# Gate and value products of an attention and gated-MLP kernel: seven block products in place of eight, on spans of 512 tokens

## The chip, the cores and the metric

The kernel runs on one core of a Trainium2 chip, as one program with one launch. Its time is device microseconds; the time before is the median of three runs, 1030.5 us (1030.05 to 1031.13). The engines of the core are named as the profile names them: PE is the matrix engine (PEld its weight loads), DVE the vector engine, ACT the scalar engine, POOL the general engine, SP the engine that issues DMAs. Each takes its own instructions in the order of the program, and waits at an instruction whose inputs or buffers aren't ready.

## The reference

```
q_s = softmax of q over head_dim;  k_s = softmax of k over the sequence
kv  = einsum('bhsd,bhse->bhde', k_s, v)            # 8 batches, 8 heads, 576 tokens, head_dim 64
x   = einsum('bhsd,bhde->bhse', q_s, kv)           # laid out as 4608 tokens x 512
out = (sigmoid(x @ w_gate) * (x @ w_val)) @ w_out  # 512 -> 1536 -> 512
```

The inputs are float32, and the three weights arrive as 64-bit floats' bit patterns and are narrowed to float32 on the chip.

## The kernel before

The 4608 tokens are worked off in 12 spans of `T = 384` (`w`), and in each span the 1536 hidden columns in 12 blocks of 128 (`j`). For a span and a block, `g1` makes gate and value of the block for all tokens of the span (two PSUM tiles `gv` of 384 columns, summed over four blocks of 128 input columns), ACT takes the sigmoid, DVE multiplies (`g_mul`), and `g2` adds the block's part of the output into one PSUM tile `acc` for each 128 tokens. `g2` of a block is issued behind `g1` of the next one.

**Split products.** From the second span on, each factor is held as two float32r parts, a rounded one (`hi`) and the rest (`lo`), and a product is three matmuls: hi by hi, lo by hi, hi by lo. The first span (w = 0) is computed in plain float32 instead, since the weights only arrive and are narrowed while it runs: `narrow_low`, `narrow_sign`, `narrow_abs`, `narrow_join` (lines 84 to 107, on DVE and ACT) for block j + 2, then `w_split` (line 128) makes its two parts, the `hi` on ACT, the `lo` on POOL. Gate and value weights then stay in SBUF in two parts for all spans. The output weights stay in float32, and `split_wo` (line 419) makes their two parts again for every span and block, ACT for `hi` (line 422), POOL for `lo` (line 423).

**Attention** of the next span is spread over the blocks of the running one by `side(n, j)` (line 502): row maxima, exponentials and sums of q (`qn_*`), q again in the other layout (`qT_*`, with maxima and reciprocals sent through DRAM and spread over partitions as `q_b`), and, if a new batch begins, `k_sub`, `k_exp`, `k_mm`, `k_done`. `x_mm` (line 362) makes the next span's x from it in three float32r matmuls for each head pair; where a span covers two batches it makes two parts, each at least 256 tokens wide, and `x_ev` (line 403) splits x into `x_hi` and `x_lo`.

The order on each engine is that of the code (`manual_schedule`): per block `g1`, `split_wo`, `g_mul`, the split of the product, `g2` of the block ahead, `side`. PSUM has eight tiles of 512 columns: three `gv`, three `acc`, two `at` for attention. With three `gv` tiles a new `g1` needs the tile that was read one block ago.

```
for s, rh in ((0, xh), (0, xl), (1, xh)):
    nc.tensor.matmul(
        ps[i], lhsT=w_hl[j][:, i, s, ks], rhs=rh[:, kt], ...
```

Of the kernel before, what the change touches and what calls it, by code (L numbers as in the profile page):

```python
# [17 lines left out]
P = 128  # L18
# [3 lines left out]
T = 384  # L22
# [4 lines left out]
NK = DM // P  # L27
G = P // H
NC = 4
# [4 lines left out]
NS = 7  # L34
EPS = 1e-9


@with_exitstack
def attn_moe(ctx: ExitStack, tc: tile.TileContext, qf, qn, qT, k, kT, v, wg, wv, wo, out):
# [15 lines left out]
    nc.vector.memset(kv_0, 0.0)
    v_ones = [const.tile([P, NP, VW], F32, name=f"v_sb{i}") for i in range(2)]
# [3 lines left out]
    ctx.enter_context(tc.manual_schedule())  # L60

# [37 lines left out]
    def narrow_abs(raw, w):  # L99
        nc.scalar.activation(w, words(raw)[:, :, 1].bitcast(F32), AF.Abs, scale=2.0 ** -112)  # L100

    def narrow_join(raw, w):
        bits = w.bitcast(I32)
        nc.vector.scalar_tensor_tensor(  # L104
            out=bits, in0=bits, scalar=3, in1=words(raw)[:, :, 0],
            op0=ALU.logical_shift_left, op1=ALU.bitwise_or,
        )

    w_32 = {}

    def w_bits(j, jo):

        raws = [w_raw[i].rearrange("p n e -> p (n e)") for i in (j,) if i in w_raw]
        raws += [wo_raw[i] for i in (jo,) if i in wo_raw]
        for f in (narrow_low, narrow_sign):
            for raw in raws:
                f(raw)

    def w_abs(j):
        w_32[j] = [ring.tile([P, DM], F32, name="ring") for _ in range(2)]  # L120
        for n in range(2):
            narrow_abs(w_raw[j][:, n], w_32[j][n])

    def w_join(j, *parts):
        for n in parts or range(2):
            narrow_join(w_raw[j][:, n], w_32[j][n])

    def w_split(j):
        w = w_32[j]
        w_hl[j] = hl = wpool.tile([P, 2, 2, DM], F32R, name="w_hl", tag=f"w{j}")  # L130
        for n in range(2):
            nc.scalar.copy(out=hl[:, n, 0], in_=w[n])  # L132
            nc.gpsimd.tensor_tensor(  # L133
                out=hl[:, n, 1], in0=w[n], in1=hl[:, n, 0].bitcast(F32), op=ALU.subtract
            )

    def wo_abs(j):
        narrow_abs(wo_raw[j], wo_32[:, j])

    def wo_join(j):  # L140
        narrow_join(wo_raw.pop(j), wo_32[:, j])
# [705 lines left out]
```

## Time and profile before

| | before |
|---|---|
| median of three runs | 1030.5 us |
| the profiled execution's own time | 1030.21 us |
| its span, first to last instruction | 1028.4 us |
| mean granted PE clock | 0.992 |
| matmuls in the profile | 5202 |
| HBM read and written | 80.87 MB and 9.70 MB |

Times inside the profile are counted from the first instruction. A matmul's duration in it is longer than the step from its start to the next one's start, because matmuls overlap; what a row of matmuls costs is read from starts. A plain float32 matmul of the code stands in the profile as two matmuls of its width. An entry such as "L443 ... gv<-x_hi,w_hl" is line 443, written tile, read tiles.

### The profile page before, as it was taken

To read this page: it belongs to the slowest core of one execution; us is meant where nothing else is said; L and a number is where in the kernel's file an instruction comes from. 1 tells how busy PE (TensorE), PEld (TensorE's weight loads), DVE (VectorE), ACT (ScalarE), POOL (GpSimd) and SP (SyncE) were. 2 spreads that over 40 slices of the span, in tenths; PEclk is the share of its full clock that TensorE was granted. 3 is DMA by queue.
4 is the path that set the end of the run, shared out by engine and by line. 5 is a ranking of instruction groups with operands and counts; after the bars stand their busy time and mean duration, and the time that the engine had idled before them with its cause. 6 is when DMAs were issued, how large, how long until landed. Compare 5 with 4: busy or idle time off the path is not lost.

```text
span 1028.4 us, 13887 instructions
## 1 busy us (share of the span) xinstructions
PE 1007.8 (98%) x5202; PEld 901.7 (88%) x5202; DVE 482.4 (47%) x835; ACT 361.0 (35%) x670; POOL 387.9 (38%) x335
## 2 busy tenths in 40 slices
PE   6988999999999999999999999999999999999998
PEld 5545579999999999999999999999999999999997
DVE  7899943435444443343353443344444443343222
ACT  3544533324324334324324232332442342332211
POOL 3346243434425523525425433334432541351221
PEclk8998999999999999999999999999999999999999
DMA  9934301233214201305315311124223420120000
GB/s 328 366 86 175 113 32 62 77 95 119 80 52 146 86 16 47 101 23 155 99 51 155 88 47 47 61 64 134 88 83 82 126 73 8 57 68 1 32 1 31
DMA packets 71746, 91.47 MB, mean 89 GB/s; under 512 B 13440, under 2 KB 53376, under 8 KB 71680
## 3 DMA queue, kind: packets, MB, share of 16 engines
q1 hardware_dynamic: 71680, 90.60, 28.0%
q8 instruction: 41, 0.67, 0.3%
q14 instruction: 25, 0.20, 0.1%
HBM read 80.87 MB, written 9.70 MB: 88 GB/s over the span
## 4 chain that ended last, share of the span: by engine, by line
PE 88%; DVE 5%; DMA 3%; issue 2%; SPq 1%; ACT 0%; DVEq 0%; ACTq 0%
PE gv L443 54%; PE acc L482 27%; PE at L207 3%; PE at L375 3%; PE gv L436 2%; DVE ring L104 1%; PE acc L476 1%; DMA x_lent<-wo_in 1%; DVE w_raw L87 1%; DMA w_raw<-wv_in 1%; DMA x_lent<-k_in 1%; SPq L185 1%; DMA lent<-k_in 0%; DVE x_lent L87 0%; DVE x_lent L94 0%
## 5 line engine op out<-in xcount | busy, mean ns | idle before, releaser
L443 PE MATMUL gv<-x_hi,w_hl 128*128 128x384 f32 x2112 | 561.9, 336 | 0.0
L443 PEld LDWEIGHTS gv<-x_hi,w_hl 128*128 128x128 f32 x2112 | 383.8, 188 | 4.4 <-issue 0.5
L423 POOL TENSOR_TENSOR wo_lo<-wo,wo_hi 128x512 fp32r<-128x512 f32 x132 | 170.2, 1289 | 520.4 <-ACT wo_hi L422 465.6
L443 PE MATMUL gv<-x_lo,w_hl 128*128 128x384 f32 x1056 | 353.8, 335 | 0.0
L454 DVE TENSOR_TENSOR sig<-gv,sig 128x384 f32<-128x384 f32 x144 | 80.4, 558 | 426.4 <-PE gv L443 421.8
L449 ACT ACTIVATE sig<-gv 128x384 f32<-128x384 f32 x144 | 70.8, 492 | 408.3 <-PE gv L443 386.2
L443 PEld LDWEIGHTS gv<-x_lo,w_hl 128*128 128x128 f32 x1056 | 198.3, 188 | 4.0 <-issue 0.5
L482 PE MATMUL acc<-wo_hi,g_lo 128*128 128x512 f32 x396 | 156.7, 396 | 0.0
L482 PE MATMUL acc<-wo_lo,g_hi 128*128 128x512 f32 x396 | 156.4, 395 | 0.0
L482 PE MATMUL acc<-wo_hi,g_hi 128*128 128x512 f32 x396 | 153.9, 389 | 0.0
L463 DVE TENSOR_TENSOR g_lo<-sig,g_hi 128x384 fp32r<-128x384 f32 x132 | 94.8, 718 | 4.6
L482 PEld LDWEIGHTS acc<-wo_hi,g_lo 128*128 128x128 f32 x396 | 74.2, 187 | 15.8
L482 PEld LDWEIGHTS acc<-wo_lo,g_hi 128*128 128x128 f32 x396 | 74.2, 187 | 12.6
L482 PEld LDWEIGHTS acc<-wo_hi,g_hi 128*128 128x128 f32 x396 | 74.4, 188 | 11.8
L422 ACT CAST wo_hi<-wo 128x512 fp32r<-128x512 f32 x132 | 80.8, 612 | 0.0
L458 DVE CAST g_hi<-sig 128x384 fp32r<-128x384 f32 x132 | 75.5, 572 | 4.6
L408 ACT CAST x_hi<-at 128x192 fp32r<-128x192 f32 (+1 forms) x60 | 23.5, 395 | 145.5 <-PE at L375 133.2
L436 PE MATMUL gv<-x,ring 128*128 128x384 f32 x192 | 63.8, 487 | 0.0
L436 PEld LDWEIGHTS gv<-x,ring 128*128 128x128 f32 x192 | 36.1, 190 | 25.3 <-issue 1.7
L133 POOL TENSOR_TENSOR w_hl<-ring,w_hl 128x512 fp32r<-128x512 f32 x24 | 37.9, 1601 | 51.6 <-ACT w_hl L132 51.6
L409 DVE TENSOR_TENSOR x_lo<-at,x_hi 128x192 fp32r<-128x192 f32 (+1 forms) x60 | 26.9, 450 | 47.9 <-ACT x_hi L408 47.9
L339 POOL TENSOR_TENSOR q_sb<-q_sb,q_b 128x384 f32<-128x384 f32 x40 | 42.3, 1075 | 9.4 <-ACT q_sb L335 8.6
(111 smaller groups left out, 822.1 us busy)
## 6 DMA issues: line engine op xcount, KB each, us to landing
out<-ring SPq DMA_DIRECT2D x36, 256.0 KB, 2.1
q_sb<-qn_in SPq DMA_DIRECT2D x40, 192.0 KB, 4.3
q_b<-q_m_row SPq DMA_DIRECT2D x80, 96.0 KB, 2.7
q_sb<-qT_in SPq DMA_DIRECT2D x40, 192.0 KB, 3.5
q_b<-q_r_row SPq DMA_DIRECT2D x80, 96.0 KB, 2.8
kT_sb<-kT_in SPq DMA_DIRECT2D x24, 288.0 KB, 3.0
v_sb<-v_in SPq DMA_DIRECT2D x26, 256.0 KB, 4.0
w_raw<-wg_in SPq DMA_DIRECT2D x12, 512.0 KB, 7.4
```

What stands on the lines that cost most here:

```text
L133: nc.gpsimd.tensor_tensor(out=hl[:, n, 1], in0=w[n], in1=hl[:, n, 0].bitcast(F32), op=ALU.subtract)
L207: nc.tensor.matmul(kvps[b, g][:, i], lhsT=kt[:n, hp * P:(hp + 1) * P], rhs=vt[:n, hp], start=(t == 0 and i == 0), stop=(t == len(KTILES) - ...
L339: eng.tensor_tensor(out=t, in0=t, in1=q_b.pop((w, "r", hp)), op=ALU.mult)
L422: nc.scalar.copy(out=oh, in_=wo_32[:, j])
L423: nc.gpsimd.tensor_tensor(out=ol, in0=wo_32[:, j], in1=oh.bitcast(F32), op=ALU.subtract)
L436: nc.tensor.matmul(ps[i], lhsT=w_32[j][i][:, kt * P:(kt + 1) * P], rhs=x_0[:, kt], start=(kt == 0), stop=(kt == NK - 1),)
L443: nc.tensor.matmul(ps[i], lhsT=w_hl[j][:, i, s, ks], rhs=rh[:, kt], start=(kt == 0 and s == 0 and rh is xh), stop=(kt == NK - 1 and s == 1),)
L449: nc.scalar.activation(sig, ps[0], AF.Sigmoid)
L454: nc.vector.tensor_tensor(out=sig, in0=val, in1=sig, op=ALU.mult)
L458: copy(out=g_hl[w, j][0], in_=gate[w, j][0])
L463: nc.vector.tensor_tensor(out=lo, in0=g, in1=hi.bitcast(F32), op=ALU.subtract)
L482: nc.tensor.matmul(acc[w][m], lhsT=lh[:, sl], rhs=rh, start=(j == 0 and lh is gh and rh is oh), stop=(j == NJ - 1 and lh is gl),)
```

## The change

Spans become 512 tokens wide (9 in place of 12; the first is still computed in float32), and from the second span on two blocks of hidden columns (a pair `p`, six for each span) are made together. Weights and x are cut into 2 by 2 blocks: two column blocks and two halves of the 512 inputs for the weights (A11, A12, A21, A22), two halves of the inputs and two halves of the tokens for x (B11, B12, B21, B22). The four results are sums of seven products of 256 inputs by 256 tokens: A11·B11, S1·T1, S2·T2, A12·B21, S3·T3, S4·B22, A22·T4, with S1 = A21 + A22, S2 = S1 − A11, S3 = A11 − A21, S4 = A12 − S2, and T1 to T4 such differences of x. Each product is three matmuls for gate and for value and each half of its inputs, so a pair has 84 matmuls of 256 columns.

- The weights' three used blocks (`a_w`) stay in SBUF in two parts. The four sums are made once, in the first span (`split_w`), stored to DRAM, and read back for every pair into one buffer `s_sb` by POOL-issued DMAs (`s_load`), each as soon as the product that used the old content is through.
- Partial results are kept in three PSUM tiles (y, z, rr), with copies on ACT (lines 604 to 614) and sums on DVE and POOL (lines 612 to 618) into `sg`. y is added to further after each copy.
- The output weights are no longer kept in SBUF in float32: `wo_dram` holds them, `wo_load` reads a pair. Their two parts (`wo_hl`) have one buffer.
- x stays in float32 in `x_32`; `c_subs` (POOL) and `c_split` (ACT and DVE) make its seven inputs at the end of a span. `x_32` also takes the output on its way to DRAM.
- The sum of k's softmax comes from an exponential of the transposed k with a running sum on ACT (`k_sum`), no longer from a column of ones in `v`.
- `x_mm` cuts at the batch border itself, parts from 64 to 448 tokens wide. Attention has one PSUM tile, `acc` four.
- In the first span the subtractions for q and k are moved from POOL to DVE, and the weights' split leaves POOL.

```diff
-T = 384
+T = 512
...
-    def w_split(j):
-        w = w_32[j]
-        w_hl[j] = hl = wpool.tile([P, 2, 2, DM], F32R, name="w_hl", tag=f"w{j}")
-        for n in range(2):
-            nc.scalar.copy(out=hl[:, n, 0], in_=w[n])
-            nc.gpsimd.tensor_tensor(
-                out=hl[:, n, 1], in0=w[n], in1=hl[:, n, 0].bitcast(F32), op=ALU.subtract
-            )
...
+    def split_w(p):
...
+        def tt(o, x, y, op):
+            nc.vector.tensor_tensor(out=o, in0=x, in1=y, op=op)
+
+        def parts(o, x):
+            nc.scalar.copy(out=o[:, :, 0], in_=x)
+            tt(o[:, :, 1], x, o[:, :, 0].bitcast(F32), ALU.subtract)
+
+        tt(t[:, S1], f[:, 2], f[:, 3], ALU.add)
+        tt(t[:, S2], t[:, S1], f[:, 0], ALU.subtract)
+        tt(t[:, S3], f[:, 0], f[:, 2], ALU.subtract)
+        tt(t[:, S4], f[:, 1], t[:, S2], ALU.subtract)
+        parts(s[:, 0:2], t[:, 0:2])
+        parts(s[:, 2:4], t[:, 2:4])
+        nc.sync.dma_start(
+            out=s_dram[p], in_=s_sb.rearrange("p s h n e -> p (s h n e)").bitcast(F32)
+        )
+        parts(a[:, A11:A12 + 1], f[:, 0:2])
+        parts(a[:, A22:A22 + 1], f[:, 3:4])
+
+    def s_load(p, i):
+        n = 4 * 2 * P
+        nc.gpsimd.dma_start(
+            out=s_sb[:, i].rearrange("p h n e -> p (h n e)"),
+            in_=s_dram[p][:, i * n:(i + 1) * n].bitcast(F32R),
+        )
...
+    def k_sum(b, hp):
+        t = kT_sb.pop((b, hp))
+        nc.scalar.activation(
+            t, t, AF.Exp, bias=kneg[b][:, hp:hp + 1], accum_out=ksum[b][:, hp:hp + 1]
+        )
...
+    def c_subs():
...
+        sub(T1, quarter(0, 1), quarter(0, 0))
+        sub(T2, quarter(1, 1), c_32[T1])
+        sub(T3, quarter(1, 1), quarter(0, 1))
+        sub(T4, quarter(1, 0), c_32[T2])
+
+    def c_split(i):
...
+        nc.scalar.copy(out=hi, in_=src)
+        nc.vector.tensor_tensor(out=lo, in0=src, in1=hi.bitcast(F32), op=ALU.subtract)
...
+        prod(y, wa(A11), B11, True, False)
+        nc.scalar.copy(out=sg[:, 0], in_=y)
+        prod(z, wsum(S1), T1, True, False)
+        nc.scalar.copy(out=sg[:, 2], in_=z)
+        more(S1)
+        prod(y, wsum(S2), T2, False, False)
+        nc.scalar.copy(out=sg[:, 1], in_=y)
+        more(S2)
+        prod(rr, wa(A12), B21, True, True)
+        nc.vector.tensor_tensor(out=sg[:, 0], in0=rr, in1=sg[:, 0], op=ALU.add)
+        prod(y, wsum(S3), T3, False, False)
+        nc.scalar.copy(out=sg[:, 3], in_=y)
+        more(S3)
+        nc.gpsimd.tensor_tensor(out=sg[:, 3], in0=sg[:, 3], in1=sg[:, 2], op=ALU.add)
+        prod(z, wsum(S4), B22, False, True)
+        nc.vector.tensor_tensor(out=sg[:, 1], in0=z, in1=sg[:, 1], op=ALU.add)
+        nc.scalar.activation(sg[:, 0:2, 0], sg[:, 0:2, 0], AF.Sigmoid)
+        more(S4)
+        prod(y, wa(A22), T4, False, True)
+        nc.scalar.activation(sg[:, 3, 0], sg[:, 3, 0], AF.Sigmoid)
+        nc.scalar.activation(sg[:, 2, 0], y[:, 0], AF.Sigmoid)
...
+    def h_split(w, p):
...
+        nc.vector.tensor_copy(out=hi, in_=sg[:, :, 0])
+        nc.vector.tensor_tensor(
+            out=lo, in0=sg[:, :, 0], in1=hi.bitcast(F32), op=ALU.subtract
+        )
...
+    def side_a(n, p):
...
+        if p == 1:
+            for c in range(NC):
+                qn_exp(n, c)
+            if b is not None:
+                k_exp(b, 0)
+                for t in range(1, 5):
+                    k_sub(b, t)
...
+                for t in range(1, 5):
+                    k_exp(b, t)
+                k_sum(b, 2); k_sum(b, 3)
...
+    def side_b(n, p):
...
+            if p == 2:
+                k_mm(b, 3); k_mm(b, 4)
+                k_done(b)
...
+            if p == 2:
+                k_max(b, 0); k_max(b, 1)
+                k_sum(b, 0); k_sum(b, 1)
...
+    for w in range(1, NW):
+        last = w == NW - 1
+        for p in range(NS):
+            end = last and p == NS - 1
+            if not end:
+                wo_load(w + (p + 1) // NS, (p + 1) % NS)
+            g1(w, p, None if end else (p + 1) % NS)
+            if p == NS - 1 and not last:
+                side_a(w + 1, p)
+                c_subs()
+                for i in range(7):
+                    c_split(i)
+            h_split(w, p)
+            if p < NS - 1 and not last:
+                side_a(w + 1, p)
+            if prev is None:
+                g2_0(NJ - 1)
             else:
+                g2(*prev)
+            split_wo(w, p)
+            prev = (w, p)
+            if not last:
+                side_b(w + 1, p)
```

Where the instructions now stand, at three places. First ACT's queue around the end of the next batch's k work (pair 2 of a span), where line 650 is the output weights' `hi`, lines 350 and 259 are `kv_split` and `k_sum`, and lines 604 to 614 are the next pair's copies. Before, at the same point of the work (`kv_hi` is line 238, sigmoid line 449):

```order
L449 ACTIVATE sig<-gv 128x384
L422 CAST wo_hi<-wo_78 128x512
L238 CAST kv_hi<-kv_f 128x256 x2
L345 CAST qT_hi<-q_sb 128x384
L449 ACTIVATE sig<-gv 128x384
```

And with the change:

```order
L442 ACT_TABLE_LOAD
L442 ACTIVATE ring<-ring 128x512 x4
L650 CAST wo_hl<-wo_t 128x1024
L350 CAST kv_sb<-kmax_b 64x4x64 x2
L259 ACTIVATE kt_86,k_sum<-kt_86,k_neg 128x576
L259 ACTIVATE kt_87,k_sum<-kt_87,k_neg 128x576
L604 COPY sg<-gv 128x512
L606 COPY sg<-gv 128x512
L609 COPY sg<-gv 128x512
L614 COPY sg<-gv 128x512
```

Two exponentials with a sum have come in behind the copies of kv, and ahead of the pair's first copy out of PSUM.

Second DVE's queue at the end of a span. Before, the last blocks of a span on DVE (line 454 is the product with the gate, 458 and 463 its two parts, 346 and 409 the rests of q and x):

```order
L346 TENSOR_TENSOR qT_lo<-q_sb,qT_hi 128x384
L409 TENSOR_TENSOR x_lo<-at,x_hi 128x384
L454 TENSOR_TENSOR sig<-gv,sig 128x384
L458 CAST g_hi<-sig 128x384
L463 TENSOR_TENSOR g_lo<-sig,g_hi 128x384
```

With the change, at the last pair of a span (lines 625 to 627 are the products with the gate, 528 the rests of the seven inputs, 637 and 638 `h_split`, 612 the next pair's first sum; buffer numbers are kept here):

```order
L627 TENSOR_TENSOR sg_82<-gv_1858,sg_82 128x256
L528 TENSOR_TENSOR c_hl_1978<-x_32_81,c_hl_1978 128x512
L528 TENSOR_TENSOR c_hl_1978<-ring_1970,c_hl_1978 128x512
L528 TENSOR_TENSOR c_hl_1983<-ring_1972,c_hl_1983 128x512
L528 TENSOR_TENSOR c_hl_1983<-x_32_81,c_hl_1983 128x512
L528 TENSOR_TENSOR c_hl_1988<-ring_1974,c_hl_1988 128x512
L528 TENSOR_TENSOR c_hl_1988<-x_32_81,c_hl_1988 128x512
L528 TENSOR_TENSOR c_hl_1993<-ring_1976,c_hl_1993 128x512
L637 CAST h_1996<-sg_82 128x1024
L638 TENSOR_TENSOR h_1997<-sg_82,h_1996 128x1024
L612 TENSOR_TENSOR sg_82<-gv_2047,sg_82 128x512
```

Seven subtractions now stand between the gate's product and the two reads of `sg` that free it.

Third POOL's queue. Before, at the start of a span's attention work (line 423 the rest of the output weights, 280, 192 and 318 subtractions for q and k):

```order
L280 TENSOR_TENSOR q_sb<-q_sb,q_m 128x384 x4
L423 TENSOR_TENSOR wo_lo<-wo_78,wo_hi 128x512
L192 TENSOR_TENSOR ring<-ring,kmax_b 128x512 x4
L423 TENSOR_TENSOR wo_lo<-wo_78,wo_hi 128x512 x3
L192 TENSOR_TENSOR ring<-ring,kmax_b 64x512
L318 TENSOR_TENSOR q_sb<-q_sb,q_b 128x384 x2
```

With the change, from the middle of pair 1 to the end of pair 2 (line 224 is `s_load`, 616 the sum into `sg`, 651 the rest of the output weights):

```order
L224 DMA s_sb<-s_92 128x1024 x3
L616 TENSOR_TENSOR sg<-sg 128x512
L224 DMA s_sb<-s_92 128x1024
L290 TENSOR_TENSOR ring<-ring,kmax_b 128x512 x3
L290 TENSOR_TENSOR ring<-ring,kmax_b 64x512
L427 TENSOR_TENSOR ring<-ring,q_b 128x512 x2
L651 TENSOR_TENSOR wo_hl<-wo_t,wo_hl 128x1024
L224 DMA s_sb<-s_93 128x1024 x3
L616 TENSOR_TENSOR sg<-sg 128x512
L224 DMA s_sb<-s_93 128x1024
```

Four DMA issues for each pair now stand in POOL's queue, each behind a product on PE, and the attention's subtractions stand between them.

More of the change, by code (lines that the diff above doesn't have):

```diff
@@ L33 @@
 NF = 2
-NS = 7
 EPS = 1e-9
+A11, A12, A22 = range(3)
+S1, S2, S3, S4 = range(4)
+B11, T1, T2, B21, T3, B22, T4 = range(7)
 @with_exitstack
@@ L197, in k_exp, with k_mm_0, k_mm @@
         nc.scalar.activation(kt[:n], kt[:n], AF.Exp)
-    def k_mm(b, t, halves=(0, 1)):
+    def k_mm_0(t, g, ps):
+        n = KTILES[t][1]
+        kt, vt = kt_sb[0, t], v_sb[0, t]
+        for i in range(2):
+            hp = 2 * g + i
+            nc.tensor.matmul(
+                ps[:, i], lhsT=kt[:n, hp * P:(hp + 1) * P], rhs=vt[:n, hp],
+                start=(t == 0 and i == 0), stop=(t == len(KTILES) - 1 and i == 1),
+                skip_group_check=True,
+            )
+    def k_mm(b, t):
@@ L236, in kv_split @@
-    def kv_split(b, gs, kv):
-        hi, lo = kv_hl[b]
-        nc.scalar.copy(out=hi[:, gs], in_=kv)
-        nc.vector.tensor_tensor(
-            out=lo[:, gs], in0=kv, in1=hi[:, gs].bitcast(F32), op=ALU.subtract
-        )
+        if t == 0:
+            kvps[b] = ps_at.tile([P, NP, P], F32, name="at")
+        for hp in range(NP):
+            sl = slice(hp * P, (hp + 1) * P)
+            nc.tensor.matmul(
+                kvps[b][:, hp], lhsT=kt[:n, sl], rhs=vt[:n, sl],
+                start=(t == 0 and hp == 0), stop=(t == len(KTILES) - 1 and hp == NP - 1),
+                skip_group_check=True,
+            )
@@ new lines, in acc_new, with acc_out, g2_0 @@
+    def acc_new(w):
+        acc[w] = [ps_acc.tile([P, DM], F32, name="acc") for _ in range(NT)]
+    def acc_out(w):
+        for m in range(NT):
+            nc.scalar.copy(out=x_32[:, m], in_=acc[w][m])
+            nc.sync.dma_start(out=out[w * T + m * P:w * T + (m + 1) * P], in_=x_32[:, m])
+        del acc[w]
+    def g2_0(j):
+        if j == 0:
+            acc_new(0)
+        for m in range(NT):
+            nc.tensor.matmul(
+                acc[0][m], lhsT=h_0[j][:, m * P:(m + 1) * P], rhs=wo_t[0, j // 2][:, j % 2],
+                start=(j == 0), stop=(j == NJ - 1),
+            )
+        if j == NJ - 1:
+            acc_out(0)
@@ L718, in attn_moe @@
         qn_exp(0, c)
-    k_exp(0, 1)
-    for t in range(2, 5):
+    for t in range(1, 5):
         k_exp(0, t)
+    kv0 = [ps_acc.tile([P, 2, VW], F32, name="acc") for _ in range(2)]
     for t in range(5):
-        k_mm(0, t, (0,))
+        k_mm_0(t, 0, kv0[0])
     for c in range(NC):
```

744 lines of the change are left out of this document (385 added, 359 removed).

## The prediction

> **What bounds the kernel now.** I read the page first: busy shares, the granted clock, the chain that ended last.
>
> ```profile
> span 1028.4 us, 13887 instructions
> PE 1007.8 (98%) x5202; PEld 901.7 (88%) x5202; DVE 482.4 (47%) x835; ACT 361.0 (35%) x670; POOL 387.9 (38%) x335
> PE 88%; DVE 5%; DMA 3%; issue 2%; SPq 1%; ACT 0%; DVEq 0%; ACTq 0%
> ```
>
> PE is busy 98% of the span and holds 88% of the chain; DVE and DMA have 8% between them, so they must bind in some stretch. The table of windows, cut at the first matmul block, at the end of the first span and at the last matmul, finds it (columns: window, its length, busy time and instructions of PE, PEld, DVE, ACT and POOL, granted clock, DMA share, GB/s):
>
> ```profile
> core 0: us, PE busy (x) PEld busy (x) DVE busy (x) ACT busy (x) POOL busy (x), PEclk, DMA share, GB/s
> 0.00:29.70 29.70, 20.47 (x111) 17.09 (x112) 21.61 (x38) 9.68 (x18) 9.91 (x18) 0.89 0.98 339
> 29.70:142.60 112.90, 105.01 (x336) 58.92 (x334) 101.93 (x131) 54.00 (x99) 52.88 (x35) 0.95 0.44 154
> 142.60:1024.50 881.90, 881.90 (x4759) 825.69 (x4758) 358.83 (x666) 296.39 (x553) 325.07 (x282) 1.00 0.24 72
> 1024.50:1028.50 4.00, 0.41 (x2) 0.00 (x0) 0.00 (x0) 0.94 (x2) 0.00 (x0) 1.00 0.53 197
> ```
>
> In the 881.9 us of the eleven split spans PE never pauses, at full clock: only PE work counts there, and any new wait is added whole. In the first span (112.9 us) DVE is busy 102 and PE idles 7.9; here DVE counts too. The execution took 1030.21 us, 1.8 more than its span, and the median of the runs is 1030.5; I sum against 1030.2.
>
> **The products.** What a matmul costs is the step between starts in the timeline of PE:
>
> ```profile
> 508.28 0.39 PE L482 MATMUL acc<-wo_hi,g_hi 128*128 128x512 f32 x1
> 510.36 0.33 PE L443 MATMUL gv<-x_hi,w_hl 128*128 128x384 f32 x1
> 514.55 0.39 PE L482 MATMUL acc<-wo_hi,g_hi 128*128 128x512 f32 x1
> 134.15 0.28 PE L375 MATMUL at<-qT_hi,kv_hi 128*128 128x256 f32 x1
> 135.10 0.28 PE L375 MATMUL at<-qT_hi,kv_lo 128*128 128x256 f32 x1
> ```
>
> From 508.28 to 510.36 are 9 steps of 512 columns, 231 ns each; from 510.36 to 514.55 are 24 of 384, 174.6 each; from 134.15 to 135.10 are 8 of 256, 118.75 each. The narrow form's two thirds would be 116.4, so it pays 2% extra. Before: 11 spans × 12 blocks × 24 = 3168 × 0.1746 = 553.1 us. After: 8 spans × 6 pairs × 84 = 4032 × 0.11875 = 478.8, so **−74.3**: 13% less: an eighth from seven for eight, 3% because 4096 tokens are left to the split spans and not 4224, and the 2% paid back. Output: 1188 matmuls of 512 become 1152, 36 × 0.231 = **−8.3**. `x_mm`, by form:
>
> ```profile
> L375 PE MATMUL at<-qT_hi,kv_hi 128*128 128x256 f32 x32 | 9.5, 296 | 0.3 <-DVE qT_lo L346 0.3
> L375 PE MATMUL at<-qT_hi,kv_hi 128*128 128x384 f32 x28 | 9.3, 333 | 0.0
> ```
>
> Three times 28 × 0.1746 + 32 × 0.119 is 26.1 us, of which 12 × 2 × 0.119 stand in the first span: 23.2 here. After, seven spans are made here in 13 parts, from 64 to 512 wide, 12 matmuls to a part. No row is narrower than 256. If narrow ones cost as much as 256 (0.119) and wide ones go by columns, it is 23 us; at twice 0.119 for the five narrow parts, 30. I take 27, **+4**, since the step from 384 to 256 already loses a little. One output block of the first span slips into this stretch, **+0.9**. Together −77.7.
>
> **The first span.** Plain float32:
>
> ```profile
> 71.73 5.32 PE L436 MATMUL gv<-x,ring 128*128 128x384 f32 x16
> 76.89 2.74 PE L476 MATMUL acc<-wo,sig 128*128 128x512 f32 x6
> 79.47 5.32 PE L436 MATMUL gv<-x,ring 128*128 128x384 f32 x16
> ```
>
> A block is 5.16 + 2.58 = 7.74 us now; 512 tokens make 24 matmuls of 512 columns at 0.43, 10.32. Twelve blocks: **+31**. DVE's side, from its timeline and groups:
>
> ```profile
> 30.45 0.70 DVE L87 TENSOR_SCALAR w_raw<-w_raw 128x1024 uint32<-128x1024 uint32 x1
> 66.10 1.32 DVE L94 TENSOR_SCALAR w_raw<-w_raw 128x1024 uint16<-128x1024 uint16 x1
> 61.24 0.42 DVE L87 TENSOR_SCALAR x_lent<-x_lent 128x512 uint32<-128x512 uint32 x1
> 61.70 0.74 DVE L94 TENSOR_SCALAR x_lent<-x_lent 128x512 uint16<-128x512 uint16 x1
> 62.54 0.69 DVE L104 SCALAR_TENSOR_TENSOR wo<-wo,x_lent 128x512 int32<-128x512 int32 x1
> L682 DVE TENSOR_TENSOR lent<-lent 128x512 f32<-128x512 f32 x2 | 1.4, 692 | 1.1 <-DMA lent<-k_in 1.0
> ```
>
> Narrowing one block is 0.70 + 1.32 + 2 × 0.69 + 0.42 + 0.74 + 0.69 = 5.2 us. `split_w` adds five instructions of 512 at 0.69 and three of 1024 at twice that, 7.6 uncontended at most. With the gate's product (0.7) and the moved subtractions of q and k (about 0.5 a block) DVE has some 14 us in the six blocks with a `split_w`; PE has 10.3 and about 1 of attention (105.0 less 12 × 7.74, over 12 blocks). Five gaps of 2.6: **+13**. The last sums are stored (2 MB), and the first reload must land before S1·T1, partly behind the last blocks; the nearest DMA rows:
>
> ```profile
> wo_raw<-wo_in SPq DMA_DIRECT2D x8, 512.0 KB, 5.0
> x_lent<-wo_in SPq DMA_DIRECT2D x4, 512.0 KB, 8.7
> ```
>
> Nothing to 12 us (a store and a load); I take one load of 5.0, **+5**. Against it the 7.9 of PE idle that DVE causes now are counted within the new bound, **−8**. The first span comes to +41, with bounds of +23 (DVE hides behind PE, as its total permits) and +58 (PE's idle stays, and the reload shows whole). More tokens before the first block, +2 (0 to 4); four tiles to copy out at the end, not three, +0.6 by a copy of 0.588:
>
> ```profile
> L491 ACT COPY ring<-acc 128x512 f32<-128x512 f32 x36 | 21.2, 588 | 26.5 <-PE acc L482 21.7 <-PE acc L476 2.5
> ```
>
> **New waits in the split spans.** In a pair, A11·B11 takes 12 × 0.11875 = 1.43 us; y is then copied by ACT, S1·T1 runs beside that, and S2·T2, which writes y again, wants to start at 2.85. From a last matmul's start to the reading instruction is 0.3 us:
>
> ```profile
> 116.83 0.28 PE L375 MATMUL at<-qT_hi,kv_lo 128*128 128x256 f32 x1
> 117.15 0.32 ACT L408 CAST x_hi<-at 128x192 fp32r<-128x192 f32 x1 [1.02 <-PE at L375]
> ```
>
> So y can be read at about 1.65, is copied by 2.25, and ACT may come at most 0.6 us late. The same spacing holds for each later use of y. What stands ahead of the first copy on ACT, by the order on it:
>
> ```profile
> L449 ACT ACT_TABLE_LOAD x23 | 29.5, 1283 | 0.4
> L197 ACT ACTIVATE ring<-ring 128x512 f32<-128x512 f32 x24 | 13.2, 620 | 0.1
> L192 POOL TENSOR_TENSOR ring<-ring,kmax_b 128x512 f32<-128x512 f32 x24 | 32.0, 1364 | 2.4 <-DMA ring<-k_in 2.3
> L163 DVE TENSOR_REDUCE kmax<-kT_sb 128x1 f32<-128x576 f32 x24 | 17.9, 746 | 36.3 <-DMA kT_sb<-kT_in 36.3
> L238 ACT CAST kv_hi<-kv_f 128x256 fp32r<-128x256 f32 x14 | 5.7, 407 | 59.1 <-DVE kv_f L229 59.1
> ```
>
> After pair 1: a table load, five exponentials, four more behind POOL's subtractions (1.36 each, POOL having issued the sums' loads first), two `k_sum`, the copies of the weights. That adds up to 20 to 21.5 us of ACT between the sigmoid and the next copy, against 19.5 of PE work: 1.5 late in six spans, **+9**. After pair 2: `k_mm` on PE (1.8 us), then by turns DVE and ACT for kv (0.4 a cast), two maxima on DVE (0.75 each), and two `k_sum` that wait for those, all ahead of y's copy: 4.9 us into the pair, not 2.85, in the five spans that begin a batch there, about 2.2 each, **+11**. After pair 5, seven `c_split` rests on DVE stand ahead of `h_split`, and the next pair's copy into the single `sg` waits for `h_split`. PE has the x product (3.4), g2 (5.5) and 2.2 of the next pair, 11 us, to cover it. DVE: rests after x (3.4 + 0.9), seven of 0.69, two of 1.2 = 11.5 to 12, if nothing slows it; POOL's `c_subs` run at the same time, and these are rows where both work:
>
> ```profile
> 173.67 2.37 POOL L318 TENSOR_TENSOR q_sb<-q_sb,q_b 128x384 f32<-128x384 f32 x2 [0.53 <-DMA q_sb<-qT_in]
> 173.91 1.25 DVE L463 TENSOR_TENSOR g_lo<-sig,g_hi 128x384 fp32r<-128x384 f32 x1
> L463 DVE TENSOR_TENSOR g_lo<-sig,g_hi 128x384 fp32r<-128x384 f32 x132 | 94.8, 718 | 4.6
> ```
>
> The subtraction took 1.25 us beside POOL's, against 0.72 in the mean. If four of seven are drawn out by 0.5 to 1 us, it is some 5 us late, not 1; between 1 and 5 I take 3.5 in seven spans, **+24.5**. Who waits behind it: ACT's copy, then S2·T2, with all of PE behind. Together +44.5, with bounds of 10 (ACT late only after pair 2) and 75 (every pair end as in the worst row).
>
> [...]
>
> **Sum.** 1030.2 − 77.7 + 41 + 2 + 0.6 + 44.5 = 1040.6; I say **1040**. The forecast is that PE loses in the first span and in waits at pair ends slightly more than the products give.
>
> **Rivals.**
> - **A, PE stays dense.** For: the 881.9 us without any PE pause, with ACT 34% and DVE 41% busy there. If the waits are only those that no order avoids (12 us) and the first span is PE-bound (+33): 1030.2 − 77.7 + 33 + 2.6 + 12 = **1000**. Against: the single `sg`, and work of other engines placed ahead of copies that PE waits for within 0.6 us.
> - **D, waits that slow the clock, too.** After an idle time of 3.15 us six matmuls took 4.54 us, not 2.74:
>
> ```profile
> 59.62 4.54 PE L476 MATMUL acc<-wo,sig 128*128 128x512 f32 x6 [3.15 <-DVE sig L454]
> ```
>
>   so an idle time over 3 us costs 1.8 more. From 5 us at each span's end and after each pair 2 (64 us of waits) with twelve such idles: 1030.2 − 77.7 + 43.6 + 64 + 21.6 = **1082**. [...]
> - **C, the sums come late.** 2 MB a pair, in four POOL-issued loads, each behind the product that frees its part. At 5.0 us one behind another it is 20 us against the pair's 15.6 (84 × 0.11875 + 24 × 0.231): 4.4 × 48 = 211 in place of 44.5, **1207**, slower than before. It decides from 2 MB per 15.6 us, 134 GB/s; the head runs at 339, so the bytes fit, and each part has most of a pair to land. What speaks for it is only that no POOL-issued load is in the trace. [...]
>
> **How the numbers follow.** Forecast 0.50 (its own range 1022 to 1058), A 0.35, D 0.10, C 0.05. The range goes from 992, in A's lower part (the bounds of 10 and +23 give 986), to 1076, into D; left out are some 0.08 below and 0.11 above. A measurement of this kernel can tell about 0.2% from no change, so 1028 to 1032.5 is the same. A lies below that, with about 0.03 of the forecast; 0.07 of it falls within; the rest, with D and C, is above. Faster 0.38, same 0.07, slower 0.55.
>
> **What would show it.** Products: steps of 119 ns between the new matmuls in a dense pair, 15.6 us from a pair to the next. First span: it ends about 184 us in (142.6 + 41), DVE busy nearly all of blocks 5 to 10. Waits: PE idle at the S2·T2 product after pairs 1, 2 and 5, released by ACT's copy, with `sg` waiting for DVE after pair 5; 1.5, 2.2 and 3.5 us. If these gaps are below 0.5, A holds. A granted clock below 1.0 in the split spans would speak for D; S products released by a DMA, for C. Wrong altogether would be the step of 119 ns, if alternating PSUM targets or weights in two parts cost more.

## The result, and the profile after

The changed kernel takes 1205.3 us (median of four runs, 1201.73 to 1206.88) where the kernel before takes 1030.4: a ratio of 1.169 (95% interval 1.166 to 1.172). My forecast was 1040. The profiled execution has a span of 1205.1 us. From its page:

```profile
span 1205.1 us, 15904 instructions
PE 1011.6 (84%) x6062; PEld 871.6 (72%) x6062; DVE 577.9 (48%) x796; ACT 482.0 (40%) x827; POOL 479.8 (40%) x450
PE 54%; DVE 18%; DMA 12%; issue 6%; POOL 4%; SPq 4%; ACT 2%; POOLq 0%; DVEq 0%; ACTq 0%
HBM read 205.13 MB, written 25.41 MB: 191 GB/s over the span
```

PE's share of the chain falls from 88 to 54%. The table of windows, cut where the one of before was (end of the head, first split product, last matmul; columns as there):

```profile
29.70:187.70 158.00, 142.45 (x378) 68.96 (x377) 133.50 (x199) 72.48 (x116) 6.97 (x4) 0.95 0.57 210
187.70:1201.00 1013.30, 849.99 (x5589) 785.86 (x5588) 419.32 (x565) 399.31 (x696) 461.07 (x430) 0.90 0.62 185
```

The first span grew from 112.9 to 158.0 us (+45.1), the split spans from 881.9 to 1013.3 (+131.4). In the latter PE is busy 850 us at a mean clock of 0.90, and idle for 163.3. What it waits for, from the view of waits (us in total, times, longest):

```profile
PE at L316 <- DMA v<-v_in: 86.2, 12, 12.8
PE gv L586 <- ACT sg L604: 47.8, 14, 6.6
PE acc L661 <- POOL wo_hl L651: 16.1, 8, 2.9
PE at L472 <- DVE ring L452: 14.1, 5, 4.9
PE gv L586 <- DMA s_sb<-s: 10.2, 1, 10.2
```

The fourth row stands in the first span; the other four, 160.3 us together, make up nearly all of the idle time of the split spans. The largest, v for k's products (line 316), is in no term of my sum. The timeline of PE in a middle span shows the places:

```profile
370.96 1.60 PE L586 MATMUL gv<-c_hl,a_w 128*128 128x256 f32 x12
375.55 1.17 PE L316 MATMUL at<-v,ring 128*128 128x128 f32 x8 [3.00 <-DMA v<-v_in]
...
378.65 7.72 PE L661 MATMUL acc<-wo_hl,h 128*128 128x512 f32 x23 [1.51 <-POOL wo_hl L651]
...
398.63 2.07 PE L316 MATMUL at<-v,ring 64*128 64x128 f32 x8 [11.37 <-DMA v<-v_in]
...
419.34 1.59 PE L586 MATMUL gv<-c_hl,a_w 128*128 128x256 f32 x12
...
429.10 0.94 PE L472 MATMUL at<-ring,kv_sb 128*128 128x192 f32 x6
...
460.48 2.93 PE L586 MATMUL gv<-c_hl,s_sb 128*128 128x256 f32 x12 [5.41 <-ACT sg L604]
463.21 2.12 PE L586 MATMUL gv<-c_hl,a_w 128*128 128x256 f32 x9
```

From 419.34 to 429.10 a pair's 84 matmuls run without a pause, 116 ns each: the products cost what the forecast says, or less. There the granted clock is 1.00. After the idle 5.41 us, twelve take 2.73 us (460.48 to 463.21) where 1.4 is usual, at a granted clock of 0.50. What the v load waited for shows in the queues of SP and POOL in the same stretch:

```profile
366.82 0.33 SPq L376 DMA_DIRECT2D q_r_row<-q_r  x1
...
369.66 1.99 SPq L423 DMA_DIRECT2D ring<-qT_in  x2
...
381.64 1.09 SPq L423 DMA_DIRECT2D ring<-qT_in  x2
393.34 2.37 SPq L416 DMA_DIRECT2D q_b<-q_r_row  x4
395.75 0.59 SPq L285 DMA_DIRECT2D v<-v_in  x1
```

```profile
373.72 2.58 POOL L427 TENSOR_TENSOR ring<-ring,q_b 128x512 f32<-128x512 f32 x2 [13.12 <-DMA ring<-qT_in]
376.25 2.35 POOL L651 TENSOR_TENSOR wo_hl<-wo_t,wo_hl 128x1024 fp32r<-128x1024 f32 x1
378.54 1.63 POOL L224 DMA_DIRECT2D s_sb<-s  x3
...
392.06 2.48 POOL L427 TENSOR_TENSOR ring<-ring,q_b 128x512 f32<-128x512 f32 x2 [10.09 <-DMA ring<-qT_in]
```

It is one chain. SP waits until 366.8 for DVE's sums of q, and only then issues q's tiles; POOL stands idle 13 us for them, with the rest of the output weights and the loads of sums queued behind it; those loads, 1.5 MB from 378.5 on, then go out together with the next q tiles, which land 10 us after their issue; SP's next spread waits for POOL's work on these tiles, and behind it, in the same queue, stands the last 128 KB of v, issued at 395.75, for which PE has waited since 387. That load itself is quick: its median from issue to landing is 2.9 us. It is issued late.

### The profile page after: what moved, and what is told of

It reads as the page before. It is cut to its first block, busy times and chain, and to the rows that moved or that the text cites. A ratio compares the mean times of both kernels' runs of the same rounds, so it can differ in the third digit from the quotient of the medians.

```text
span 1205.1 us, 15904 instructions
## 1 busy us (share of the span) xinstructions
PE 1011.6 (84%) x6062; PEld 871.6 (72%) x6062; DVE 577.9 (48%) x796; ACT 482.0 (40%) x827; POOL 479.8 (40%) x450
## 4 chain that ended last, share of the span: by engine, by line
PE 54%; DVE 18%; DMA 12%; issue 6%; POOL 4%; SPq 4%; ACT 2%; POOLq 0%; DVEq 0%; ACTq 0%
PE gv L586 31%; PE acc L661 13%; DMA ring<-qT_in 7%; DVE c_hl L528 5%; PE gv L543 4%; SPq L416 3%; DVE sg L625 3%; DMA v<-v_in 2%; PE at L472 2%; PE at L316 2%; POOL wo_hl L651 2%; DVE sg L626 1%; POOL ring L427 1%; DVE h L638 1%; PE acc L568 1%
## 5 line engine op out<-in xcount | busy, mean ns | idle before, releaser
L586 PE MATMUL gv<-c_hl,s_sb 128*128 128x256 f32 x2304 | 297.4, 286 | 58.0 <-ACT sg L604 47.8
L586 PEld LDWEIGHTS gv<-c_hl,s_sb 128*128 128x128 f32 x2304 | 286.6, 197 | 60.9 <-ACT sg L604 50.6
L661 PE MATMUL acc<-wo_hl,h 128*128 128x512 f32 x1152 | 291.5, 410 | 17.2 <-POOL wo_hl L651 16.1
L661 PEld LDWEIGHTS acc<-wo_hl,h 128*128 128x128 f32 x1152 | 226.2, 199 | 67.7 <-POOL wo_hl L651 19.2
L586 PE MATMUL gv<-c_hl,a_w 128*128 128x256 f32 x1728 | 247.3, 296 | 0.0
L586 PEld LDWEIGHTS gv<-c_hl,a_w 128*128 128x128 f32 x1728 | 233.1, 203 | 4.0 <-issue 1.8
L224 POOL DMA_DIRECT2D s_sb<-s x192 | 106.0, 553 | 199.8 <-PE gv L586 179.7
L651 POOL TENSOR_TENSOR wo_hl<-wo_t,wo_hl 128x1024 fp32r<-128x1024 f32 x48 | 118.3, 2465 | 110.4 <-issue 87.2
L316 PE MATMUL at<-v,ring 128*128 128x128 f32 (+1 forms) x256 | 40.5, 313 | 87.4 <-DMA v<-v_in 86.2
L625 DVE TENSOR_TENSOR sg<-sg 128x512 f32<-128x512 f32 x48 | 68.7, 1432 | 33.5 <-ACT sg L619 33.5
L543 PE MATMUL gv<-x,f_w 128*128 128x512 f32 x160 | 73.7, 616 | 0.0
```

Of the source, the lines that this page charges most:

```text
L224: nc.gpsimd.dma_start(out=s_sb[:, i].rearrange("p h n e -> p (h n e)"), in_=s_dram[p][:, i * n:(i + 1) * n].bitcast(F32R),)
L316: nc.tensor.matmul(kvps[b][:, hp], lhsT=kt[:n, sl], rhs=vt[:n, sl], start=(t == 0 and hp == 0), stop=(t == len(KTILES) - 1 and hp == NP - ...
L543: nc.tensor.matmul(ps[n], lhsT=w[:, kt // 2, sl], rhs=x_0[:, kt], start=(kt == 0), stop=(kt == NK - 1),)
L586: nc.tensor.matmul(ps[:, n], lhsT=lh(kt), rhs=c_hl[i][:, x, kt], start=(first and n == 0 and kt == 0 and lh is wh and x == 0), stop=(last ...
L625: tt(out=sg[:, 0:2, 0], in0=sg[:, 0:2, 0], in1=sg[:, 0:2, 1], op=ALU.mult)
L651: nc.gpsimd.tensor_tensor(out=lo, in0=src, in1=hi.bitcast(F32), op=ALU.subtract)
```

## The experiments

Each time is of a single run unless an interval is given. The runs were made on several chips, on which the kernel before takes 1029.5 to 1033.7 us, and four runs of one kernel lie up to 5 us apart, in one case 13; differences of that size are not read. Theories: Q, the order in the queues; B, the bytes of the reloaded sums; H, `h_split`'s place.

**The last part of v earlier.**

```diff
         if p == 2:
+            if b is not None:
+                k_mm(b, 2)
+                v_load(b, 4)
             q_spread(n, "m", 2); q_spread(n, "m", 3)
...
-            if b is not None:
-                k_mm(b, 2)
-                v_load(b, 4)
```

> The load of the last part of v (64 rows) and the k product that frees its buffer are put ahead of q's spread maxima in pair 2, so that this load no longer stands on SP behind the reciprocals' spread, which waits for POOL. Theory Q (the 86.2 us of PE waiting for v are SP's order): the wait of some 11.5 us after pair 2 goes in seven spans, 80 us, and perhaps 10 more as PE keeps its clock: 1110 to 1130. Theory B (v is late because 2 MB of sums a pair slow every transfer): the load is issued 17 us earlier but the q transfers that follow stay slow, and the wait only turns into one for another transfer: above 1170.

Measured: 1190.4. The view of waits:

```profile
PE gv L586 <- ACT sg L604: 106.0, 15, 11.7
PE acc L661 <- POOL wo_hl L651: 16.9, 8, 3.2
PE at L316 <- DMA v<-v_in: 16.2, 6, 3.5
```

The wait for v went as Q says (86.2 to 16.2), but 58 us of it came back as waits for ACT's copy, and the time is the one that B gave. ACT's exponential of the second q tiles waits for POOL, POOL waits 10.6 us for these tiles, and the copy is queued behind it: a second branch of the same chain, and, as B said, a wait for another transfer. Whether the order or the bytes made that transfer late, this run doesn't tell.

**A sixteenth of the sums' bytes.**

```diff
-            out=s_sb[:, i].rearrange("p h n e -> p (h n e)"),
-            in_=s_dram[p][:, i * n:(i + 1) * n].bitcast(F32R),
+            out=s_sb[:, i].rearrange("p h n e -> p (h n e)")[:, 0:n // 16],
+            in_=s_dram[p][:, i * n:i * n + n // 16].bitcast(F32R),
```

> Each load of sums reads back a sixteenth of its columns (32 KB in place of 512), at the same places in the queues; the other columns keep the sums of the last pair, so the products are not the right ones. Theory Q: the long PE wait for v stays in each span, shorter by what the transfers in the chain land faster (q's tile took 9 us to land here, would take 3): 4 to 7 us left in each span, 1205 - 35 - 10 for the first load = 1150 to 1170. Theory B: the waits for v fall under 2 us a span, and the time to about 1100.

Measured: 1161.4. The waits for v are 51.2 us, two in a span, that for the last part 5 to 6 us each. The second pair of q tiles landed after 5 us, not 10. So Q, and the bytes (B) are worth 44 us.

**`h_split` ahead of the seven splits.**

```diff
             if p == NS - 1 and not last:
                 side_a(w + 1, p)
+                h_split(w, p)
                 c_subs()
                 for i in range(7):
                     c_split(i)
-            h_split(w, p)
+            else:
+                h_split(w, p)
```

> At the last pair of a span h_split is put ahead of the seven splits of the next inputs. Theory H (the 5.5 us wait for ACT's copy after pair 5 is the place of h_split behind seven rests on DVE): that wait goes in seven spans, 1205 - 39 = 1166, or somewhat less with the clock. Rival: the splits, pushed back 2 us, are late themselves, and PE waits as long at the products that read them: 1195 to 1205.

Measured: 1170.2. Waits for the copy fell from 47.8 to 13.7 us, and waits for the split inputs came up, 12.7 in 13 places. H, with 35 of the 39 us.

**Both.**

> The early load of v and h_split ahead, together. Theories Q and H: the two gains add, 1070 to 1090. Rival (each wait hides the other, since one span's end gives the next its slack): clearly less than the sum of the two single gains.

Measured: 1151.0. The single gains (15 and 35) add, to 54; the expected 1070 to 1090 is missed because the wait for v had only moved.

**q's chain earlier.** (`ring` has 11 buffers, not 9.)

```diff
         if p == 1:
+            q_spread(n, "m", 0); q_spread(n, "m", 1)
+            qT_load(n, 0); qT_load(n, 1)
             for c in range(NC):
                 qn_exp(n, c)
...
-            q_spread(n, "m", 0); q_spread(n, "m", 1)
...
-            qT_load(n, 0); qT_load(n, 1)
             qT_sub(n, 0); qT_sub(n, 1)
```

> The first two of q's spread maxima and of its tiles in the other layout are issued at the head of pair 1, ahead of the store of q's sums, which waits for DVE (two more ring buffers, so that the tiles need not wait for the old q tiles). Theory Q2 (the whole stop after pairs 1 and 2 is one chain: sums of q on DVE, SP's queue, q's tile, POOL's subtraction, and behind that the weights' rest, the loads of sums, v): POOL's 13 us idle at line 427 go, PE's waits for v and wo_hl fall from 102 us to under 30: 1090 to 1115. Rival B2 (every transfer is slow beside the sums' reload, whatever the order): the second q tile still takes 9 to 10 us to land and the waits for v keep half their length: above 1145.

Measured: 1156.3. The waits for `wo_hl` fell to 2.0 us, those for v to 71.4, one a span: the chain's first half went (49 us with the clock, whose mean over the profiled run went from 0.904 to 0.922), the second, through the second q tiles, stayed. Time and waits are those that the rival gave; but the edit moved the first half alone, so it doesn't show that order has no part in the second.

**These three together, and again with a sixteenth of the bytes.**

> q's chain early, v's last part early, and h_split ahead of the splits. Theories Q2 and H: 1060 to 1085, and no PE wait over 3 us left in a middle span. Rival (the sums' transfers bind by themselves): above 1110, with waits for s_sb or q tiles in the middle spans.

> The three fixes, with each load of sums reading back a sixteenth of its columns (the products are not the right ones). Theory M (mixed: the bytes of the sums slow q's tile, 10 us from issue to landing, and the engines' orders pass that on to PE): the tile lands in about 4 us, PE's wait after pair 2 (11.2 us at the third product, behind ACT) falls to about 5: 1110 - 7 x 6 - 5 = 1060 to 1070. Rival Q3 (only orders): within 10 us of 1110. Rival B3 (only bytes): the wait goes altogether, 1035 or less.

Measured: 1109.9 and 1083.9, both above what theories Q2, H and M gave. In the first, v costs 6.7 us, but the third product after pair 2 waits 11.2 us in this middle span:

```profile
498.06 2.93 PE L586 MATMUL gv<-c_hl,s_sb 128*128 128x256 f32 x12 [11.19 <-ACT sg L604]
```

```profile
489.74 0.63 ACT L442 ACTIVATE ring<-ring 128x512 f32<-128x512 f32 x1 [9.30 <-POOL ring L427]
...
497.44 0.56 ACT L604 COPY sg<-gv 128x512 f32<-128x512 f32 x1
```

```profile
488.45 2.48 POOL L427 TENSOR_TENSOR ring<-ring,q_b 128x512 f32<-128x512 f32 x2 [10.68 <-DMA ring<-qT_in]
```

With a sixteenth of the bytes the q tiles land in 4.2 us (median), not 10.1, and the waits for the copy go from 63.5 to 46.8. Of these 46.8, some 20 are new: after pair 1 the copy now waits 3.4 us in each of six spans, there for `h_split` on DVE. So the bytes are worth 26 us of the time (about 21 when each run is set against the kernel before on its own chip), and the other waits stand without them.

**q's second half a pair later.** Its loads stand at the end of pair 1, its subtraction on POOL behind pair 2's rest of the output weights, its exponential in pair 3. (The spread of the reciprocals and the multiplications by them move back with it; those lines are left out here.)

```diff
         if p == 2:
...
-            qT_sub(n, 2); qT_sub(n, 3)
-            for hp in range(NP):
-                qT_exp(n, hp)
+            qT_exp(n, 0); qT_exp(n, 1)
...
         if p == 3:
+            qT_exp(n, 2); qT_exp(n, 3)
...
+        if p == 1:
+            q_spread(n, "m", 2); q_spread(n, "m", 3)
+            qT_load(n, 2); qT_load(n, 3)
+        if p == 2:
+            qT_sub(n, 2); qT_sub(n, 3)
```

> On top of the three fixes, the second half of q's other layout is loaded at the end of pair 1 and worked on a pair later: its subtraction on POOL stands behind the weights' rest of pair 2, its exponential on ACT in pair 3. Theory O (ACT's exponential, waiting for POOL and that for the tile, holds up kv, the sums of k and the first copy of the next pair, all behind it on ACT): the 11 us after pair 2 fall to the 2 of my forecast: 1110 - 63 - 8 = 1035 to 1050. Rival: the wait moves to the x products of pair 3, less than 25 us gained.

Measured: 1076.0. The waits for the copy are 2.6 us in all, as O says; but PE waits 33.9 for v again, six times, up to 8.3: its 128 KB, issued at 467.6 in one span, were used at 479.6, beside 2 MB of sums issued from 465.8 to 469.5. Such a load lands 10.8 us after its issue here (median of six), 2.9 in the changed kernel.

**The last part of v in its own buffer**, loaded in the span before.

```diff
-                v_load(b, 0); v_load(b, 1)
+                v_load(b, 0); v_load(b, 1); v_load(b, 4, v_4)
```

> On top of the kernel with q's second half later, the last part of v has a buffer of its own and is loaded with the first two at the end of the span before. Theory M (what is left, 33.9 us of PE waiting for v, is this load of 128 KB landing 12 us after its issue, behind 2 MB of sums issued within 3 us): all of it goes, 1076 - 34 - 5 = 1035 to 1042. Rival: another transfer of the same stretch becomes the wait, above 1055.

Measured: 1056.8; no wait for v is left, and waits for the copy are back at 18.7 us, nearly all of it five of 3.6 to 3.9. Theory M for the load; the rival for half of the gain.

**The first span.** Three edits were tried alone: the sums on POOL, and the rests of the weights' blocks on POOL with the last store in four parts; and the store's place on SP, this one too with the last store in four parts (left out here):

```diff
-        if j + 4 < NJ:
-            load_wo(j + 4)
-        if j + 6 < NJ:
-            load_w(j + 6)
+        if j < 5:
+            load_wo(j + 4)
+            load_w(j + 6)
...
         after_first(j)
+        if 5 <= j < 8:
+            load_wo(j + 4)
+        if j == 5:
+            load_w(j + 6)
```

> In the first span the four sums of weight blocks of each pair are formed on POOL, not DVE (7 us of POOL in place of 2.8 of DVE; POOL is idle there). Theory S (DVE is the bound in the six blocks with sums, so that x's product waits 13.4 us for q's rest): these waits shrink below 4, the last store goes out some 3 us earlier: 1205 - 10 - 5 = 1185 to 1192. Rival: POOL's reads hold up DVE's two-input operations, and ACT's rounding waits for POOL: no gain, 1200 to 1210.

> The changed kernel with two edits in the first span alone: the rests of the weights' own blocks (nothing on DVE waits for them) are made on POOL, not DVE, and the last pair's sums are stored in four parts, so that the first reload waits for a quarter. Theory S2: PE's waits for q's rest fall from 13.4 to about 6, and the wait for the first sums from 10.2 to about 5: 1205 - 12 = 1190 to 1195. [...]

> The changed kernel with SP's order in the first span alone changed: from block 5 on the weights' loads of later blocks stand behind the store of the sums (the first store stood 6.5 us behind a load that waited for DVE), and the last store goes out in four parts. Theory SP (the x waits of 13.4 us come from the single s_sb, whose store was late: ACT's rounding waited 7.3 us for it and DVE 8.3 us for ACT; and the wait for the first sums is the store's 7.4 us plus the load's): x waits under 7, first sums under 6: 1205 - 11 = 1190 to 1196. Rival (DVE's own work is the bound, as I forecast): 1200 to 1206, since DVE's work is the same.

Measured: 1218.5, 1205.8 and 1192.2. The first two edits gained nothing; they move DVE's work to POOL, which then works beside DVE, and the x waits grow (23.9 and 17.9 us; 14.1 in the changed kernel). The store's place gained: x waits 10.8 (theory SP gave under 7), first sums 6.3, not 10.2, and the first split product starts at 177.8, not 187.7. The four parts alone aren't the reason: with them the second edit's first sums still waited 10.1. The reason is in these rows of the changed kernel:

```profile
123.19 1.99 ACT L207 CAST s_sb<-s 128x1024 fp32r<-128x1024 f32 x2 [7.32 <-DMA s<-s_sb]
```

```profile
111.80 0.42 SPq L216 DMA_DIRECT2D s<-s_sb  x1
```

```profile
124.27 2.36 DVE L204 TENSOR_TENSOR s_sb<-s,s_sb 128x1024 fp32r<-128x1024 f32 x2 [8.31 <-ACT s_sb L207]
```

DVE had finished the sums in `s_sb` at 105.3; their store stood behind a weights' load that waited, so the single `s_sb` came free late, and ACT (7.32 us) and DVE (8.31) stood still. With the store moved this stop is gone, and PE's waits for q's rest in the first span are 4.50, 0.65, 1.92 and 2.30 us, where they were 4.51, 4.91, 0.66 and 3.29. What is left, 9.4 us, stands behind DVE's own work: ahead of the longest of these waits DVE runs without a pause from 99.7 to 113.3. Beside the other edits the first two gained nothing either:

> The three and the sums on POOL. If they add: 1045 to 1070, still slower than before (1030), since the wider first span and the first reload stay. Rival: below 1030, if the clock, freed of the long idles, gives back more than the waits themselves.

> All of these edits together, without the cut in the sums. If the gains add: 1025 to 1040, about the time before; the rest against the forecast's best case is PE's clock and the 35 us by which the first span's float32 blocks are longer.

Measured: 1119.9 (three fixes: 1109.9) and 1081.3 (q's second half later: 1076.0; too small a difference for single runs).

**All that helped, and two more orders.** "All_but_sub" has everything so far, with the first input's split ahead of `h_split`; "all" moves POOL's first subtraction for q behind the rest of the output weights.

> The last kernel with both edits of the first span, and the split of the first input ahead of h_split (12 us of PE waiting for it). If they add: 1038 - 11 - 8 = 1015 to 1025, below the time before.

> The same, with POOL's first subtraction for q in pair 1 behind the rest of the output weights, so that the loads of sums are not issued in a burst after it. Theory M: the sums of pair 3 are issued as their products end, transfers land sooner, the time is the same or up to 8 us less than without this edit: 1010 to 1025. Rival: x comes late, 1030 or more.

Measured: 1056.6, and 1045.0 (ratio 1.013, interval 1.010 to 1.016). Of the expected sum the first span came (it ends at 177.5 and 176.7 us, not 188.7), the rest not: splitting the first input first made the waits for inputs longer (18.7 and 18.6 us; 13.9 with the order before), and 20.7 and 19.2 us of waits for the copy after pair 2 stayed. PE's waits are the same in both kernels within 2 us, and one of the four runs of "all" took 1054.1, so whether its own edit gained anything stays open. In "all":

```profile
463.63 0.75 DVE L260 TENSOR_REDUCE k_max<-kt 128x1 f32<-128x576 f32 x1 [0.71 <-DMA kt<-kT_in]
...
464.49 0.74 DVE L260 TENSOR_REDUCE k_max<-kt 128x1 f32<-128x576 f32 x1
```

```profile
464.61 0.78 ACT L267 ACTIVATE kt<-kt,k_neg 128x576 f32<-128x576 f32 x1 [3.67 <-DVE k_neg L261]
...
466.23 0.56 ACT L612 COPY sg<-gv 128x512 f32<-128x512 f32 x1
```

The copy of y (line 612 here) stands behind two sums of k, and these behind the maxima: the wait that I had forecast after pair 2. The last two kernels put the first input's split behind `h_split` again, move the two sums of k into pair 3 (`k_sum_two` makes those two of the next batch that aren't made yet), and in the second also form the differences of x on DVE:

```diff
         if p == 3:
...
             qT_split(n, 0); qT_split(n, 1)
+            k_sum_two(n)
...
                 k_max(b, 0); k_max(b, 1)
-                k_sum(b, 0); k_sum(b, 1)
-                kT_load(b, 2); kT_load(b, 3)
+            if p == 3:
+                k_sum_two(n)
+                kT_load(b, 2); kT_load(b, 3)
...
-                h_split(w, p)
-                c_subs()
+                c_subs(nc.vector)
+                h_split(w, p)
```

> The kernel with all edits, except that the first input's split stands behind h_split again (ahead of it, it cost 6 us more), and that the next batch's first two exponentials of the transposed k stand on ACT in the middle of pair 3, no longer behind kv at the end of pair 2. Theory W (my forecast's second wait: the copy of y after pair 2 stands behind maxima, kv and these exponentials; 2.4 us in seven spans, 18.7 us of waits for ACT): that wait goes, 1045 - 18 - 6 - 4 = 1014 to 1025, below the time before. Rival: kv_split alone keeps the copy as late, since kv waits for the last k product: 1035 or more.

> The same, with the four differences of x at a span's end on DVE, ahead of h_split, not on POOL. Theory L (DVE's two-input operations take 1.4 to 1.8 us, not 0.7, while POOL forms them): DVE has 2.8 us more work and loses 3 to 4 us of holding up; PE's waits for the split inputs (12 us) halve: 5 to 8 us less than without this edit. Rival: DVE is later by the added work, 5 us more.

Measured: **1007.9** (ratio 0.977, interval 0.975 to 0.980) and **993.6** (0.962, 0.960 to 0.964), in four runs each: the change, with its instructions in another order and three more small buffers, beats the kernel before by 3.8%. Its windows, from the first split product to the last:

```profile
179.10:989.50 810.40, 793.58 (x5590) 738.00 (x5588) 426.37 (x594) 418.77 (x712) 423.02 (x402) 1.00 0.76 231
```

PE is dense at full clock again, though the same 2 MB of sums are read for every pair. Theory W holds, with more gain than it gave, 37 us between the medians: waits for the copy fall from 19.2 to 1.7, those for inputs from 18.6 to 13.0, and the mean granted clock rises from 0.961 to 0.986 (in the two profiled runs, 47 us apart, since that of "all" is its slowest). Theory L holds too, with 14 us where it gave 5 to 8: waits for the inputs fall from 13.0 to 1.2 us, and though DVE has the differences to form, at 0.68 or 0.69 us each, the products ahead of them take 0.69 and 0.42 us at a span's end (282.60 and 283.21), where in "all", beside POOL's subtractions, they took 1.79 and 1.51 (509.38 and 511.09).

## Why the prediction was wrong

**Where the time went.** The split spans' work is 793.6 us by the last row, 88.3 below the 881.9 of before. In the changed kernel the same work is busy for 850.0, at a granted clock of 0.90 where the last row has 1.00: 56.4 us of slower matmuls. So: +45.1 (first span) − 88.3 (work) + 56.4 (clock) + 163.3 (idle) = 176.5, against 176.7 between the two spans.

**The products were right**: 116 ns a step against 118.75, and −88 for the split spans' work against −77.7.

**The first span was nearly right in size, in part in its cause.** I forecast +43 with head and first reload; it is +45.1, and 10.2 more for the reload, 55 where the bounds ended at 62 (the bound of +58 is 2 more than its terms, 31 + 13 + 12, give). The x waits of 13.4 us are near my 13, but the step "Five gaps of 2.6" has DVE's work alone as their cause. With the store moved on SP 9.4 of them are left, and these are DVE's work; the others came from the store, which no step has. That the two together meet 13 is luck. For the first reload I took one load of 5.0; it is a store of 2 MB and then the load, 10.2.

**The step that failed is "New waits in the split spans".** It gives 44.5 us for waits at three places, with 75 as the bound, where PE idles for 163.3. It follows ACT's queue to the first copy and DVE's to `h_split`, and nowhere follows SP's. There a store that waits for DVE's sums stood ahead of q's tiles before the change as well; new is that two more loads of v stand behind both, and its last load behind a spread that waits for POOL. The chain from there cost 86.2 (v) and 16.1 (`wo_hl`) directly; taken apart, it came out in turn at v, at ACT's copy and again at v, until each branch was moved. The step "each part has most of a pair to land" asked the sums to be in time for their own products. They are: in the split spans only the first one is late. What they delay is other transfers: with the three fixes, q's tiles land in 4.2 us with a sixteenth of these bytes and in 10.1 with all. That rival C's number (1207) is near the result is chance; its mechanism, late sums, has one row of 10.2 us.

**The single waits.** After pair 1: +9 forecast, and no copy was late in the changed kernel. After pair 2: +11 forecast, five of 2.2; hidden in the changed kernel behind the longer chain, it stood there once that was gone, five of 3.6 to 3.9, and went when the sums of k were moved. After pair 5: +24.5 forecast, 5.4 in each of seven spans, 38; the mechanism was right, the size that of the bound of 5, with DVE held up more than I took:

```profile
429.31 0.69 DVE L625 TENSOR_TENSOR sg<-sg 128x512 f32<-128x512 f32 x1 [0.70 <-ACT sg L619]
429.92 0.42 DVE L626 TENSOR_TENSOR sg<-sg 128x256 f32<-128x256 f32 x1
...
446.08 1.79 DVE L625 TENSOR_TENSOR sg<-sg 128x512 f32<-128x512 f32 x1 [0.70 <-ACT sg L619]
447.79 1.51 DVE L626 TENSOR_TENSOR sg<-sg 128x256 f32<-128x256 f32 x1
...
454.45 2.84 DVE L528 TENSOR_TENSOR c_hl<-x,c_hl 128x512 fp32r<-128x512 f32 x1
```

```profile
446.01 1.30 POOL L513 TENSOR_TENSOR ring<-x 128x512 f32<-128x512 f32 x1
...
453.85 2.89 POOL L651 TENSOR_TENSOR wo_hl<-wo_t,wo_hl 128x1024 fp32r<-128x1024 f32 x1 [1.68 <-ACT wo_hl L650]
```

Beside POOL's subtractions two of the gate's products take 1.79 and 1.51 us; a pair earlier, where POOL does no arithmetic, 0.69 and 0.42. The forecast slows four of the seven rests alone, and only by `c_subs`: it has neither these products nor the rest of 2.84 us beside POOL's rest of the output weights. Why DVE's instructions are drawn out there, no run here shows.

**The clock** was in rival D alone, 1.8 us for each of twelve idles. The sum has no term for it: "any new wait is added whole" counts the idle time and not the slower matmuls behind it. It came to 56.4 us: in the split spans PE has 18 idles of 3 us or more and five more stops of 2.95 to 4.8 us, four of these in two pieces; so 18 to 23, not 12, and 56.4 spread over them is 2.5 to 3.1 us each. In rival D's row the granted clock was 0.62 (59.62 to 64.16, 1.00 over the usual six); in the changed kernel it is 0.50 over the twelve matmuls that take 2.73 us, not 1.4, after 5.41 idle. How long an idle it takes doesn't come out of these runs. D's "over 3 us" rests on its one row, and at 1026.08, after an idle of 2.95 us, 23 output matmuls take 8.07 us at a granted clock of 0.62, where 24 take 5.47 elsewhere (340.17 to 345.64).

## What to carry to other kernels

Follow each queue that issues transfers as closely as the engines: where an issue waits for an engine, ask which unrelated loads stand behind it, and who waits for those. A reload that is in time for its own reader can still slow the transfers issued beside it (with the three fixes q's tiles landed in 10.1 us, with a sixteenth of the reload's bytes in 4.2); load small tiles that are needed soon before it (with the last part of v loaded a span earlier, its 33.9 us of waits went, and the time fell from 1076.0 to 1056.8). (Whether it helps to space its issues, no run here shows.) Where several waits stand in one chain, the removal of one shows the next, so a change is judged only when its order has been worked through: this one goes from 17% slower to 3.8% faster without a product or a byte of sums less.

## What the hardware showed unexpectedly

- A load of 128 KB landed 10.8 us after its issue (median of six, q's second half later) beside 2 MB of sums issued within 4 us; in the changed kernel, where no sums were issued beside it, after 2.9. With 32 KB loads in place of 512 KB ones, the 256 KB tiles of q landed in 4.2 us, not 10.1 (medians, with the three fixes).
- The loads issued by POOL cost POOL about 0.55 us each (106.0 us for 192) and landed in 6.3 us (median, 512 KB); none held up a product in a middle span.
- Float32r matmuls of 256 columns with a new weight block each step by 116 ns in a dense pair of the changed kernel; those of 512 by 231 in the kernel before.
